# Retention and SwiGLU on one core: a new order for the first batch's transposes and first weights, and six pieces behind each plain down step

## The chip, the core and the metric

The kernel runs on one core of one Trainium2 chip. A core has five engines, each with its own instruction queue: PE (TensorE, matmuls, with a weight load PEld that overlaps them), DVE (VectorE), ACT (ScalarE), POOL (GpSimd) and SP (SyncE, which here only issues DMAs). ACT issues DMAs too. The metric is the device time of one execution in microseconds (us); lower is better.

## The reference

All matrices are float32 but for the three weights, which arrive as float64.

```python
# q, k, v: (8 batches, 8 heads, 576 positions, 64)
scores = (1 / sqrt(64)) * q @ k.transpose(0, 1, 3, 2)
gamma = 1 - 2.0 ** (-5 - arange(8))                  # one decay for each head
Dmat = where(rel >= 0, gamma ** rel, 0)              # rel = query position - key position
ret = (scores * Dmat) @ v
x = ret.transpose(0, 2, 1, 3).reshape(4608, 512)     # tokens x (heads * 64)
g, val = x @ w_gate, x @ w_val                       # 512 -> 1536, each
out = (g * sigmoid(g) * val) @ w_out                 # 1536 -> 512
```

## The kernel before, in words

**Retention.** A unit of work `i` is one pair of heads of one batch (32 units; the first batch is units 0 to 3, and `HP` is 4). Its 576 positions are nine chunks of 64. Inside a chunk the scores are made, masked by `near` and multiplied with v; this is `own_values` (L519). What lies before a chunk comes in as a 64x64 state for each head: `new_states` (L529) makes each chunk's contribution from keys and values on PE, `states` (L573 to L580) chains them on DVE, and `earlier_values` (L540, L544) multiplies the states with the queries. Both kinds of value go to the PSUM tile `outer`; `to_x` (L595, L609) multiplies them out of it into the FFN's input. `masked(i)` returns three closures: `copies` (ACT copies half of the states, `even`), `own` (DVE masks the scores into `ret`) and `states`.

**Transposes.** Scores need q and k with the head dimension on the partitions. For the first batch PE does that: `transposes(i)` turns q into `bankA` and k into `bankB` by four 128x128 transposes each (L464), and the last 64 positions of both into `bankC` (L468). DVE (unit 0) or ACT (units 1 to 3) copies them out to `qT` and `kT` (L465, L471). Then `keys` (L496, L498) scales k in place, which `new_states` needs: on DVE for unit 0, on ACT for unit 1, on POOL for units 2 and 3. Later units are transposed on DVE (`STREAM_TRANSPOSE`, L481). For units 10 and 11 `keys` is on DVE.

**The order of the first batch.** `tick(t, 0, HP)` does, for t = 0 to 5: scores and new states of unit t-1 and their masks; own values, earlier values and `to_x` of unit t-2; then the transposes of unit t. Engines run their queues in the order in which the program issues (a manual schedule).

**Weights.** Each weight block is loaded raw as 64-bit words (`load_w`, L383, L385; 1 MB, three buffers), split by two ACT instructions into its high and low words (`split`, L402, L403) and rounded to float32 by two DVE instructions (`rounding`, L415, L416). `halves` lists the half blocks in the order in which they are rounded; `rounding(j)` issues `split(j+1)` behind itself, and a split of a block's second half issues the load that takes its buffer. Loads 0 to 4 are issued by SP, later ones by ACT. Block 0 is w_gate's and block 1 w_val's for the output blocks 0 and 1, so that the first projection `up0(0)` needs the first halves of both and `up0(1)` the second halves.

**FFN.** The first tile has 512 tokens and plain matmuls: `up0(f)` (L690) for f = 0 to 11, a gate bank and a value bank each, with SiLU on ACT (L694) and the product on DVE (L695); then `down0(f)` (L702) in the order `down_order`. Four more tiles of 1024 tokens follow, in which each quarter of a product is 26 block products by a bilinear scheme (tables UP, DOWN, OUT_SUMS); the sums of blocks that it needs are made on DVE and POOL (L726, through the helper `add`), and some go out to DRAM as DMAs (L777).

**Pieces.** From unit 4 on, `tick` issues the PE work at once and queues the work of the other engines as closures in `pieces`; `go_on(n)` issues the next n. While the plain down steps run, ticks 10, 11 and 12 are queued behind steps m = 1, 3 and 6, one piece is issued at once, and each further step issues five. For ticks 10 and 11 the list is: copies; outputs; own; states; transpose of q; transpose of k; `keys` of units 10 and 11. Behind the pieces, each step issues a group of sums on POOL (`groups`) and one on DVE (`last_groups`).

Of the kernel before, what the change touches and what calls it, by code (L numbers as in the profile page):

```python
# [12 lines left out]
F32 = mybir.dt.float32  # L13
# [141 lines left out]
def kernel(  # L155
# [34 lines left out]
    B, H, S, D = q.shape  # L190
    NT, DM = out.shape
    DF = moe_w_gate.shape[1]
    P = 128
    HP = H // 2
    L = D
    NC = S // L
    NFULL = S // P
    CW = NFULL * P
# [18 lines left out]
    qp = ctx.enter_context(tc.tile_pool(name="qp", bufs=2))  # L217
# [149 lines left out]
        weights.append((src, [w_dn[:, u // 2, 2 * (u % 2) + f].rearrange("p d x -> p (d x)") for f in range(2)]))  # L367
    order = [0, 1, 2, 3, 4, 5, 6, 12, 7, 8, 13, 9, 10, 14, 11, 15, 16, 17]
    assert sorted(order) == list(range(len(weights)))
    halves = [(i, f) for i in order for f in range(2)]  # L370
    RAWS = 3
    raws, parts = {}, {}

    def load_w(m):

        i, queue = order[m], nc.sync if m < 5 else nc.scalar
        raw = rest[:, raw_at + m % RAWS * 2048 : raw_at + (m % RAWS + 1) * 2048]
        raws[i] = raw.bitcast(I32)
        dst, src = raw.bitcast(I64), weights[i][0]
        if i < NUP:  # L380
            dst = dst.rearrange("p (c n) -> p c n", n=2 * P)
            for cols in (ts(0, P), ts(1, P)) if m < 2 else (slice(0, 2 * P),):
                queue.dma_start(out=dst[:, :, cols], in_=src[:, :, cols])  # L383
        else:
            queue.dma_start(out=dst.rearrange("p (f n) -> p f n", f=2), in_=src)  # L385
# [7 lines left out]
    def split(j):  # L393

        i, f = halves[j]
        bits = bits_of(i, f)
        top, ulp = [rest[:, part_at + 512 * (2 * n + j % 2) : part_at + 512 * (2 * n + j % 2 + 1)] for n in range(2)]  # L400
        blocks = lambda a: a.rearrange("p (c m) -> p c m", m=P)
        nc.scalar.activation(out=blocks(top), in_=bits[:, :, :, 1].bitcast(F32), func=AF.Prelu, scale=2.0 ** -112, alpha=2.0 ** 32)  # L402
        nc.scalar.activation(out=blocks(ulp.bitcast(I32)), in_=bits[:, :, :, 0].bitcast(U32), func=AF.Copy, scale=2.0 ** -29)  # L403
        parts[j] = top.bitcast(I32), ulp.bitcast(I32)
        if f and j // 2 + RAWS < len(order):
            load_w(j // 2 + RAWS)

    def rounding(j):

        i, f = halves[j]
        dst = weights[i][1][f].bitcast(I32)
        top, ulp = parts.pop(j)
        nc.vector.tensor_scalar(out=dst, in0=top, scalar1=3, scalar2=None, op0=ALU.logical_shift_left)  # L415
        nc.vector.tensor_tensor(out=dst, in0=dst, in1=ulp, op=ALU.add)  # L416
        if j + 1 < len(halves):
            split(j + 1)

    for m in range(RAWS):  # L420
        load_w(m)

    kT = const.tile([P, S], F32, name="kT")
    state = const.tile([P, NC, D], F32, name="state")
# [2 lines left out]
    spare = rest[:, dn_at + 2560 : sum_at]  # L427
    other = (spare[:, 0:CW].rearrange("p (h c i) -> p h c i", h=2, i=L), spare[:, CW : CW + L],
             spare[:, 640 : 640 + NC * D].rearrange("p (c d) -> p c d", d=D))
    for t in (state, other[2]):  # L430
        nc.gpsimd.memset(t[:, 0], 0.0)

# [19 lines left out]
    def transposes(i):  # L452
        p = i % HP
        qk, kn, vt = loaded.pop(i)
        qT = qp.tile([P, S], F32, tag="qT", name="qT")
        st[i] = dict(qT=qT, kn=kn, v=vt)
        pieces = []

        copy = nc.scalar.copy if i else nc.vector.tensor_copy
        if i < HP:  # L460

            for t, src, bank in ((qT, qk, bankA), (kT, kn, bankB)):
                for c in range(NFULL):
                    nc.tensor.transpose(bank[:, ts(c, P)], src[:, ts(c, P)], ident)  # L464
                copy(t[:, 0:CW], bank)  # L465
            for n, src in enumerate((qk, kn)):
                for hl in range(2):
                    nc.tensor.matmul(bankC[half[hl], ts(n, L)], src[half[hl], CW : CW + D], ident[half[hl], half[hl]],  # L468
                                     start=True, stop=True, skip_group_check=True)
            for n, t in enumerate((qT, kT)):  # L470
                copy(t[:, CW:S], bankC[:, n * L : (n + 1) * L])  # L471
        else:
            if light(i):
                def scale_q():

                    src = qk[:, 0].rearrange("p (j r) d -> p r j d", r=2)
                    for r in range(2):
                        nc.scalar.activation(out=src[:, r], in_=src[:, r], func=AF.Copy, scale=piece[:, 2 * p + r : 2 * p + r + 1])
                pieces.append(scale_q)
            for n, t in enumerate((qT, kT)):  # L480
                pieces.append(lambda n=n, t=t: nc.vector.transpose(out=t, in_=qk[:, n].rearrange("p j d -> p (j d)")))  # L481

        every = slice(0, P)

        def keys():
            blocks = kn.rearrange("p (g d) -> p g d", d=D)
            if i < HP:
                parts = [(0, every, blocks[:, 0 : NC - 1 : 2]), (1, every, blocks[:, 1:NC:2]), (1, half[1], blocks[half[1], NC - 1])]
            elif whole(i):
                parts = [(0, every, blocks[:, 0:NFULL]), (1, every, blocks[:, NFULL:NC])]  # L490
            else:
                parts = [(hl, every, blocks[:, hl : 2 * NFULL : 2]) for hl in range(2)]
            for hl, rows, at in parts:
                scale = key[rows, 2 * p + hl : 2 * p + hl + 1]
                if vector(i) or 1 < i < HP:
                    (nc.vector if vector(i) else nc.gpsimd).tensor_scalar(out=at, in0=at, scalar1=scale, scalar2=None, op0=ALU.mult)  # L496
                else:
                    nc.scalar.activation(out=at, in_=at, func=AF.Copy, scale=scale)  # L498

        if light(i):  # L500
            return [lambda: (keys(), pieces[0]())] + pieces[1:]
        if vector(i) and i:
            return [lambda: None] + pieces + [keys]
        return [keys] + pieces
# [131 lines left out]
    def tick(t, lo=HP, hi=NP, spread=False, then=None):  # L636
        go_on(len(pieces))
        if hi == HP:

            if lo <= t - 1 < hi:  # L640
                scores(t - 1, True)
                new_states(t - 1)
                for f in masked(t - 1):
                    f()
            if t == 3:
                split(0)
                rounding(0)
            if lo <= t - 2 < hi:
                own_values(t - 2)
                earlier_values(t - 2)  # L650
                to_x(t - 2)[0]()
            for f in transposes(t) if lo <= t < hi else ():
                f()
            return
        if lo <= t - 2 < hi:
            own_values(t - 2)
        if lo <= t - 1 < hi:
            new_states(t - 1)
        if lo <= t - 2 < hi:
            earlier_values(t - 2)  # L660
        if lo <= t - 1 < hi:
            scores(t - 1, t - 2 < lo)
        if lo <= t - 1 < hi and whole(t - 2) and not whole(t - 1):
            decay(slice(0, H), slice(0, H), half[1])
        copies, *masks = masked(t - 1) if lo <= t - 1 < hi else (lambda: None,)
        keys, *new = transposes(t) if lo <= t < hi else (lambda: None,)
        outputs = to_x(t - 2)[0] if lo <= t - 2 < hi else lambda: None
        if t - 2 >= 0 and light(t - 2):
            pieces.append(lambda: (copies(), keys(), outputs()))
        else:  # L670
            pieces.extend([lambda: (copies(), keys()), outputs])
        pieces.extend(masks)
        pieces.extend(new)
        if then:
            pieces.append(then)
        if not spread:
            go_on(len(pieces))

    def go_on(n):
        for _ in range(min(n, len(pieces))):  # L680
            pieces.pop(0)()
# [303 lines left out]
    for t in range(HP + 2):  # L985
        tick(t, 0, HP)

        for j in {3: (1, 2), 4: (3, 4, 5)}.get(t, ()):
            rounding(j)
        if t == 3:  # L990
            load(HP)
        if t > 3:
            for f in range(2):
                up0(f, range(2) if t == 4 else range(2, HP))
    load(HP + 1)


# [36 lines left out]
    tick_at = {1: 10, 3: 11, 6: 12, 8: 13}  # L1034
    for m, f in enumerate(down_order):
        down0(f)
        go_on(5)
        if m in tick_at:
            tick(tick_at[m], HP, FIRST, tick_at[m] + 1 < needed(1))
            go_on(1)  # L1040
        if m == 8:
            first_sums(0, 0, 4)
        if m > 8:
            x_sums(1, 3 * (m - 9), min(3 * (m - 8), X_FIRST), True)
        if groups:
            groups.pop(0)[1]()
        if last_groups:
            last_groups.pop(0)()
# [58 lines left out]
```

## Time and profile before

| what | value |
|---|---|
| median of 4 runs | 1066.01 us (1064.81 to 1067.23) |
| the profiled execution | 1065.88 us |
| its span, first to last instruction | 1064.1 us |
| PE busy | 1039.0 us (98%) |
| DVE, POOL, ACT busy | 663.2, 390.0, 273.7 us |
| first transposes on PE start | 4.17 us |
| plain up projections `up0` | 30.64 us to about 129 us |
| plain down steps `down0` | 129.24 us to about 187 us |
| mean granted TensorE clock | 0.998 |

Read it so: a row of the timeline gives the start and the duration of a group of like instructions on one engine; in brackets stands how long the engine was idle before it and what released it. The view of waits sums these for each pair of waiting and releasing instruction (us in total, times, the longest). "SPq" and "ACTq" are instructions that issue DMAs. A PE row's end is modelled: it holds the last matmul's way through the array, so that rows of work in sequence overlap a little.

### The profile page before, as it was taken

Reading aid. Unit: us, or ns where it says so; the run is one execution under the profiler, and the core shown is the slowest. Engines: PE = TensorE matmul, PEld = TensorE weight load, DVE = VectorE, ACT = ScalarE, POOL = GpSimd, SP = SyncE. Lnnn points to the kernel's source line nnn. Section 1 sums busy time; section 2 is a strip of 40 time slices with the busy share of each in tenths; the row PEclk is TensorE's granted clock in tenths of the full one; section 3 lists DMA queues with packets and bytes.
Section 4 is the critical chain, followed back from the end, with each engine's and each line's share of the span. In section 5 each row is a group of like instructions: output and inputs, shape, how many; then the busy total and the mean of one; then the engine's idle time right before and its main releaser. Section 6 shows DMA issues by size and latency. Waiting matters only on the chain.

```text
span 1064.1 us, 21426 instructions
## 1 busy us (share of the span) xinstructions
PE 1039.0 (98%) x8448; PEld 851.3 (80%) x8448; DVE 663.2 (62%) x1094; ACT 273.7 (26%) x579; POOL 390.0 (37%) x338
## 2 busy tenths in 40 slices
PE   6999989999999999999999999999999999999998
PEld 5554545888887888888888888888888888888887
DVE  5568778886878678463557778526375554244644
ACT  4456400333433210332322112232220022222110
POOL 2002356656455206621224037512250384122505
PEclk9999999999999999999999999999999999999999
DMA  9898788746768968756766867554554555555553
GB/s 272 212 281 231 195 240 227 218 143 191 187 178 217 263 166 230 212 154 182 192 161 192 220 190 212 155 151 137 151 176 155 155 179 157 150 154 160 182 159 98
DMA packets 305083, 199.09 MB, mean 187 GB/s; under 512 B 219992, under 2 KB 248664, under 8 KB 304984
## 3 DMA queue, kind: packets, MB, share of 16 engines
q1 hardware_dynamic: 269528, 157.19, 54.0%
q10 hardware_dynamic: 35456, 40.54, 11.3%
q8 instruction: 67, 1.10, 0.4%
q14 instruction: 32, 0.26, 0.1%
HBM read 157.56 MB, written 40.11 MB: 186 GB/s over the span
## 4 chain that ended last, share of the span: by engine, by line
PE 84%; DVE 8%; DMA 2%; issue 2%; POOL 1%; ACT 0%; ACTq 0%; DVEq 0%; POOLq 0%
PE bankC L919 11%; PE bankE L919 11%; PE bankB L919 11%; PE bankA L919 11%; PE bankA L958 6%; PE bankB L958 6%; PE bankE L958 6%; PE bankC L958 6%; DVE rest L859 3%; PE bankA L690 2%; PE outer L544 2%; PE bankC L690 2%; PE bankE L690 2%; PE bankB L690 2%; DVE rest L726 2%
## 5 line engine op out<-in xcount | busy, mean ns | idle before, releaser
L859 POOL TENSOR_TENSOR rest<-rest 128x512 f32<-128x512 f32 x56 | 79.2, 1420 | 298.5 <-DVE rest L859 277.5
L934 ACT ACTIVATE io<-rest 128x256 f32<-128x256 f32 x180 | 75.0, 417 | 342.3 <-DVE rest L859 294.2
L919 PE MATMUL bankC<-rest,arena 128*128 128x256 f32 x544 | 129.2, 380 | 0.5 <-DVE rest L859 0.5
L919 PE MATMUL bankA<-rest,arena 128*128 128x256 f32 x544 | 129.0, 380 | 0.6 <-DVE rest L859 0.6
L726 POOL TENSOR_TENSOR arena<-arena 128x512 f32<-128x512 f32 (+1 forms) x72 | 114.1, 1597 | 32.2 <-DMA up<-arena 21.0
L919 PE MATMUL bankE<-rest,arena 128*128 128x256 f32 x512 | 121.4, 380 | 0.6 <-DVE rest L859 0.6
L919 PE MATMUL bankB<-rest,arena 128*128 128x256 f32 x512 | 121.5, 380 | 0.4 <-DVE rest L859 0.4
L919 PEld LDWEIGHTS bankA<-rest,arena 128*128 128x128 f32 x544 | 102.9, 190 | 16.1 <-issue 1.4
L919 PEld LDWEIGHTS bankC<-rest,arena 128*128 128x128 f32 x544 | 102.8, 190 | 15.6 <-issue 1.2
L941 POOL TENSOR_TENSOR arena<-rest,io 128x256 f32<-128x256 f32 x72 | 52.0, 729 | 166.6 <-ACT io L934 166.6
L919 PEld LDWEIGHTS bankE<-rest,arena 128*128 128x128 f32 x512 | 96.9, 190 | 14.5 <-DVE rest L859 1.0
L919 PEld LDWEIGHTS bankB<-rest,arena 128*128 128x128 f32 x512 | 96.9, 190 | 14.5 <-DVE rest L859 0.8
L726 POOL TENSOR_TENSOR rest<-rest 128x256 f32<-128x256 f32 (+1 forms) x66 | 66.1, 1022 | 102.5 <-DVE rest L416 59.9
L859 DVE TENSOR_TENSOR rest<-bankC,rest 128x512 f32<-128x512 f32 x72 | 48.9, 687 | 65.4 <-PE bankC L919 45.1
L859 DVE TENSOR_TENSOR rest<-bankB,rest 128x512 f32<-128x512 f32 x72 | 48.9, 687 | 64.3 <-PE bankB L919 49.3
L859 DVE TENSOR_TENSOR rest<-bankE,rest 128x512 f32<-128x512 f32 x72 | 48.8, 686 | 63.6 <-PE bankE L919 45.4
L859 DVE TENSOR_TENSOR rest<-bankA,rest 128x512 f32<-128x512 f32 x72 | 48.8, 686 | 63.5 <-PE bankA L919 46.2
L937 DVE SCALAR_TENSOR_TENSOR arena<-rest,io 128x256 f32<-128x256 f32 x84 | 57.4, 688 | 11.7 <-ACT io L934 11.7
L958 PE MATMUL bankA<-arena 128*128 128x256 f32 x252 | 58.0, 380 | 1.4 <-DVE arena L726 1.4
L958 PE MATMUL bankB<-arena 128*128 128x256 f32 x252 | 58.3, 381 | 0.0
L958 PE MATMUL bankC<-arena 128*128 128x256 f32 x252 | 58.1, 380 | 0.0
L958 PE MATMUL bankE<-arena 128*128 128x256 f32 x252 | 57.9, 379 | 0.0
(180 smaller groups left out, 1632.5 us busy)
## 6 DMA issues: line engine op xcount, KB each, us to landing
arena<-up SPq DMA_DIRECT2D x234, 256.0 KB, 2.6
arena<-dn SPq DMA_DIRECT2D x104, 384.0 KB, 3.1
up<-arena ACTq DMA_DIRECT2D x78, 256.0 KB, 3.0
out_dram<-rest SPq DMA_DIRECT2D x32, 256.0 KB, 3.7
qk<-in_q_dram SPq DMA_DIRECT2D x108, 72.0 KB, 2.6
qk<-in_k_dram SPq DMA_DIRECT2D x108, 72.0 KB, 2.3
dn<-rest SPq DMA_DIRECT2D x52, 128.0 KB, 2.4
rest<-in_moe_w_out_dram ACTq DMA_DIRECT2D x6, 1024.0 KB
```

The lines of the kernel that those rows point to most:

```text
L544: nc.tensor.matmul(xr[half[hl]] if c + 1 == NC else xo[half[hl ^ c % 2 * exchange(i)], c // 2, c % 2], state[half[hl], c, :], s["qT"][half ...
L690: nc.tensor.matmul(bank, w_up[:, f // 4, gv, f % 4, c // 2, (c % 2) * P : (c % 2 + 1) * P], xs[0][:, c, :], start=(c == 0), stop=(c == HP ...
L726: eng.tensor_tensor(out=dst, in0=srcs[0], in1=srcs[1], op=ALU.add if op[0] == "add" else ALU.subtract)
L859: eng.tensor_tensor(out=at(op[1]), in0=at(op[2]), in1=at(op[3]), op=ALU.add if op[0] == "add" else ALU.subtract)
L919: nc.tensor.matmul(b[:, gv * TB : (gv + 1) * TB], w[:, gv, ts(c, P)], rhs[:, c, :], start=(opens and gv == 0 and c == 0), stop=(c == 1), s ...
L934: nc.scalar.activation(out=s, in_=src[:, 0:TB], func=AF.Silu, scale=-1.0 if negative else 1.0)
L937: return lambda: nc.vector.scalar_tensor_tensor(out=dst, in0=src[:, TB : 2 * TB], scalar=-1.0, in1=s, op0=ALU.mult, op1=ALU.mult)
L941: nc.gpsimd.tensor_tensor(out=dst, in0=src[:, TB : 2 * TB], in1=s, op=ALU.mult)
L958: nc.tensor.matmul(b[:, m * TB : (m + 1) * TB], lhs[:, qd, ts(m, P)], w[:, qd], start=(opens and qd == 0 and m == 0), stop=(qd == NQ - 1), ...
```

## The change

Three things are changed, and nothing is added to what is computed.

1. *The first batch's ticks.* The transposes of unit t now stand between own values and earlier values of unit t-2. For units 1 to 3, k is transposed and copied ahead of q, and each tensor's last 64 positions follow its own 128x128 transposes. The first four `qT` have places of their own (`early`) in a part of `rest` that is not yet in use.
2. *The first two weight blocks.* They are loaded and rounded by columns: first half of gate, first half of value, then the two second halves. The roundings are spread otherwise over the ticks (0 at t = 3; 1 between `own` and `states` of t = 4; 2 behind t = 4; 3, 4, 5 behind t = 5; before: 0, 1, 2 at t = 3 and 3, 4, 5 at t = 4). `up0(0)` has its first two input chunks behind t = 4 and the other two behind t = 5; `up0(1)` then runs whole. Loads 3 and 4 are tied to the splits of the second halves; on SP's queue they now come behind the ten DMAs of `load(4)`, unit 4's q, k and v, which they were ahead of.
3. *The plain down steps* issue six pieces each instead of five.

```diff
-    halves = [(i, f) for i in order for f in range(2)]
+    halves = [(i, f) for f in range(2) for i in order[0:2]] + [(i, f) for i in order[2:] for f in range(2)]
...
-    def load_w(m):
+    def load_w(m, parts=range(2)):
...
-            for cols in (ts(0, P), ts(1, P)) if m < 2 else (slice(0, 2 * P),):
+            for cols in [ts(f, P) for f in parts] if m < 2 else (slice(0, 2 * P),):
...
-        if f and j // 2 + RAWS < len(order):
-            load_w(j // 2 + RAWS)
+        m = j + 1 if 1 < j < 4 else j // 2 + RAWS
+        if f and m < len(order):
+            load_w(m)
...
-    for m in range(RAWS):
-        load_w(m)
+    for f in range(2):
+        for m in range(2):
+            load_w(m, (f,))
+    load_w(2)
...
+    early = [spare[:, 640 + S * (1 + i) : 640 + S * (2 + i)] for i in range(HP)]
...
-        qT = qp.tile([P, S], F32, tag="qT", name="qT")
+        qT = early[i] if i < HP else qp.tile([P, S], F32, tag="qT", name="qT")
...
-            for t, src, bank in ((qT, qk, bankA), (kT, kn, bankB)):
+            for n, (t, src, bank) in enumerate(((kT, kn, bankB), (qT, qk, bankA)) if i else ((qT, qk, bankA), (kT, kn, bankB))):
                 for c in range(NFULL):
                     nc.tensor.transpose(bank[:, ts(c, P)], src[:, ts(c, P)], ident)
-                copy(t[:, 0:CW], bank)
-            for n, src in enumerate((qk, kn)):
                 for hl in range(2):
                     nc.tensor.matmul(bankC[half[hl], ts(n, L)], src[half[hl], CW : CW + D], ident[half[hl], half[hl]],
                                      start=True, stop=True, skip_group_check=True)
-            for n, t in enumerate((qT, kT)):
-                copy(t[:, CW:S], bankC[:, n * L : (n + 1) * L])
+                copy(t[:, 0:CW], bank)
+                copy(t[:, CW:S], bankC[:, ts(n, L)])
...
-                for f in masked(t - 1):
-                    f()
-            if t == 3:
-                split(0)
-                rounding(0)
+                copies, own, states = masked(t - 1)
+                copies()
+                own()
+                if t == HP:
+                    rounding(1)
+                states()
             if lo <= t - 2 < hi:
                 own_values(t - 2)
+            for f in transposes(t) if lo <= t < hi else ():
+                f()
+            if lo <= t - 2 < hi:
                 earlier_values(t - 2)
                 to_x(t - 2)[0]()
-            for f in transposes(t) if lo <= t < hi else ():
-                f()
...
-        for j in {3: (1, 2), 4: (3, 4, 5)}.get(t, ()):
+        if t == 3:
+            split(0)
+        for j in {3: (0,), 4: (2,), 5: (3, 4, 5)}.get(t, ()):
             rounding(j)
         if t == 3:
             load(HP)
-        if t > 3:
-            for f in range(2):
-                up0(f, range(2) if t == 4 else range(2, HP))
+        if t == 4:
+            up0(0, range(2))
+    up0(0, range(2, HP))
+    up0(1, range(HP))
...
         down0(f)
-        go_on(5)
+        go_on(6)
```

## The prediction

> **What bounds the kernel now.** I read the busy shares first, then the view of waits for PE, then windows for the clock, then the timelines of the two places that the change touches.
>
> ```profile
> span 1064.1 us, 21426 instructions
> ...
> PE 1039.0 (98%) x8448; PEld 851.3 (80%) x8448; DVE 663.2 (62%) x1094; ACT 273.7 (26%) x579; POOL 390.0 (37%) x338
> ```
>
> PE is busy for all but 25 us. So only what shortens PE's own gaps, or makes its matmuls faster, can count. PE's waits in full come to under 20 us, and these are the ones that the change can reach:
>
> ```profile
> PE inner L529 <- DVE kn L496: 3.3, 3, 2.6
> PE inner L529 <- POOL rest L496: 2.3, 2, 1.6
> ...
> PE bankE L552 <- ACT kT L471: 1.6, 3, 0.6
> ```
>
> The first lies in the plain down steps, the other two in the first batch: new states wait for scaled keys, scores for the copies of the transposes. A wait can also cost clock:
>
> ```profile
> 25.54:28.95 3.41, 1.74 (x78) 1.47 (x74) 2.45 (x6) 2.49 (x5) 1.74 (x2) 0.99 0.99 351
> 28.95:32.37 3.42, 3.42 (x36) 2.40 (x33) 3.28 (x12) 0.72 (x2) 0.00 (x0) 0.51 1.02 340
> 32.37:35.78 3.41, 3.41 (x9) 1.52 (x8) 2.69 (x5) 2.80 (x5) 0.00 (x0) 1.00 0.90 123
> ```
>
> Columns: stretch, its length, busy time of PE, PEld, DVE, ACT, POOL, granted clock, DMA share, GB/s. After a stretch in which PE worked 1.74 of 3.41 us, the clock was 0.51 for 3.42 us. The rest of the run shows no other such dip.
>
> **The first batch, part by part.** The timeline of the third tick and the fourth:
>
> ```profile
> 18.24 0.27 PE L552 MATMUL bankE<-qT,kT 64*64 64x64 f32 x2 [0.58 <-ACT kT L471]
> ...
> 19.82 0.63 PE L529 MATMUL inner<-v,rest 64*64 64x64 f32 x27 [0.67 <-POOL rest L496]
> ...
> 24.83 0.27 PE L552 MATMUL bankE<-qT,kT 64*64 64x64 f32 x2 [0.58 <-ACT kT L471]
> ...
> 27.43 0.63 PE L529 MATMUL inner<-v,rest 64*64 64x64 f32 x27 [1.59 <-POOL rest L496]
> ```
>
> *Removed.* Transposes now come before earlier values, so that 0.33 + 0.93 us of PE work (L540, L544) stands between the last transpose and the scores. The ACT copies end about 0.75 us after the last transpose; that work hides them, and two waits of 0.58 go: 1.16. Were it gone, they would be back.
>
> POOL starts `keys` when k's transposes end. Unit 2's scaling took 17.39 to 19.77 (2.38 us for three instructions). Now k is transposed right behind own values of unit 0, which end near 14.8: its four transposes end 0.66 later, POOL runs 15.5 to 17.9, and PE reaches the new states near 14.8 + 1.7 (transposes) + 1.25 (earlier values) + 0.55 (scores) = 18.3. No wait: 0.67 goes. For unit 3 the same sum from own values ending at 19.4 gives POOL 20.1 to 22.5 and PE at 22.9: 1.59 goes. The old row for unit 3 is 3.35 us, beside rounding on DVE from 23.5 on, which now begins after `to_x` of unit 1, near 23.2. With 3.35 PE would wait 0.6; I take 2.38, the row without rounding, and keep 0.6 for the range.
>
> [...] The old rows show the stretch only beside rounding, so my sum leaves it out.
>
> Earlier values wait until own values have left the array (0.21 us between PEld rows, twice in ticks 2 and 3); transposes now fill that: 0.4.
>
> *The clock.* PE's hole at 25.84 to 27.43 closes, so the half-clock stretch should go. Its price: L544 took 1.71 us on the chain against 0.93 later, and the first four rows of `up0` 2.72 against 1.72 for the next four: 1.7 to 1.8; I take 1.7. Bounds: 0 if any 3.4 us stretch stays as empty as that one, 1.8 if not. The stretch 18.7 to 22.1 was some 0.66 busy and caused no dip, and every new stretch from 14 us on comes out above that, so I take the full value.
>
> [...]
>
> *Added.* The last 64 positions of the second tensor go into the bank that the first one's copy has to leave, and in the changed program PE waits for it: ACT's 0.49 + 0.22 behind the first transposes, against 0.5 of transposes that cover it: 0.2 in each of ticks 1 to 3, and earlier values are queued behind it: 0.6. No row shows this wait; bounds 0 to 1.5 (three times 0.5, both tensors' copies in full). In tick 0 k's copy comes behind q's small one: 0.2.
>
> *First weights.* `up0(0)` and `up0(1)` keep their matmuls. Between own values of units 2 and 3 stand now 3.44 us of `up0` instead of 6.88. In that time DVE has to do the mask (0.6), rounding 1 (1.1), the states (2.0) and `to_x` (0.85) = 4.55, against PE's own values 0.6 + earlier values 1.1 + 3.44 = 5.15, with ACT's copy of 0.4 ahead: cover 0.2. ACT's two splits stand ahead of that copy, up to 1.2 us. I charge 0.4, bounds 0 to 1.4. The DMA of gate's and value's first halves comes in the order of use; ACT splits at 21 us in both.
>
> SP passes `load(4)` ahead of load 3. SP was free at 18.67 and `load(4)` took 27.93 to 39.34 = 11.4 us to issue; from 18.7 that is 30.1, and a weight load of 1 MB took 5.6 to 6.1 us to land: near 36. Its split, behind which the first SiLU is queued on ACT, then takes 2 x 0.6, the table load 1.28, SiLU 0.60, DVE's product 0.69: 39.8, and `up0(2)` needs that bank near 43.3. Cost 0, with 3.5 us of cover.
>
> Sum: 1.16 + 0.67 + 1.59 + 0.4 + 1.7 - 0.6 - 0.2 - 0.4 = **4.3 us** saved. `up0(2)` starts at 43.5 instead of 47.82. From there to 129 us PE shows no wait, and each engine's queue hangs on PE as before. Ends: 1.1 (no clock, added terms at their bounds) to 5.7.
>
> **Six pieces.** The timeline of DVE, then of PE, around unit 10's keys:
>
> ```profile
> 144.95 0.73 DVE L481 STREAM_TRANSPOSE kT<-qk 128x576 f32<-128x576 f32 x1
> 145.61 2.98 DVE L726 TENSOR_TENSOR rest<-rest 128x256 f32<-128x256 f32 x4
> 148.51 1.64 DVE L496 TENSOR_SCALAR kn<-kn,tab 128x256 f32<-128x256 f32 x2
> ```
>
> ```profile
> 146.08 0.69 PE L519 MATMUL outer<-ret,v 64*64 64x64 f32 x32
> 149.38 0.33 PE L529 MATMUL inner<-v,kn 64*64 64x64 f32 x2 [2.60 <-DVE kn L496]
> 150.21 0.63 PE L529 MATMUL inner<-v,kn 64*64 64x64 f32 x27 [0.51 <-DVE kn L496]
> ```
>
> Four sums stand between the transpose and the keys. The sixth piece is `keys`, so it changes places with them: it starts at 145.6 instead of 148.5, 2.9 us sooner, and PE gets its keys at 147.3 instead of 150.2. What is late next is still `keys`, by 0.7 against a pass without wait. For unit 11 three sums (2.13 us) step aside; own values to L540 took 1.75 there against 0.98 in the tick at 126.5, so 0.8 goes. The sums now delay DVE's `even` copy: they end at 150.2, PE has its states ready at 149.6, and PE does not need that copy's results before 160. The sums' DMAs to DRAM leave ACT's queue 1.6 us later; the later tiles fetch them only behind their up steps. POOL's groups keep their places. Tick 12 has four pieces and is untouched. Sum 2.9 + 0.8 = **3.7 us**; with DVE slowed by POOL 2.6, at most 4.3 (all delay of the two passes).
>
> **Where it could leak.** In 190 to 290 us PE has waits of 0.3 to 0.8 us for DVE and POOL, so DVE must come early too. It does: it idles 2.42, 1.75 and 0.92 us for PE at 152.6, 166.6 and 176.0, the last just before it starts the first big tile's sums. POOL idles 3.3 us at 177.8. I charge 0, with 2 us as the bad end.
>
> Total 4.3 + 3.7 = 8.0. The profiled execution is 1065.88, span 1064.1; so 1065.88 - 8.0 = **1057.9 us** (span 1056.1). The median of the runs is 0.13 above the profiled one, which I neglect.
>
> **Rivals.**
> *Half of the first batch's gain is lost:* the clock dips again and own values of unit 3 wait for `to_x`. The cover of 0.2 us speaks for it; the closed hole against. Gain 1.1 to 2.6 + 3.7: 1059.6 to 1061.1, middle 1060.4. Chance 0.17.
> *The shift does not pass the first big tile:* DVE or POOL there set the end. Their bracketed waits for PE speak against. If half of the gain stays behind: 1062; if nearly all, no change. Chance 0.10.
> *Slower: load 3 late.* SP's waits show one DMA of a later unit standing 9.9 us behind a weight load. If `load(4)` stands so ahead of load 3, that lands near 46.5; PE stalls from 39.5 on, by 7 us, and a hole of that length brings half clock for one or two stretches, 1.7 to 3.4 more. From a landing at 47.5 on, the stall alone eats the whole gain. 1057.9 + 7.0 + 3.4 = 1068.3. Against it: no ACT-issued load stands among the DMAs that load 3 follows. Chance 0.05.
> The forecast itself: 0.68.
>
> **How the numbers follow.** A measurement of this kernel tells 0.2% (2.1 us) from no change. Faster: 0.68 + 0.17 + 0.06 of the second rival's 0.10 (most of the ways to split it lie beyond 2.1 us) = 0.91; same 0.04 (the rest of it); slower 0.05. The forecast's own spread is +-2 (1.1 for added waits, 0.6 for keys, 1 for the six pieces), 1055.9 to 1059.9; with the first rival's whole span and part of the second the range is 1055.4 to 1061.4.
>
> **What would show it.** Right: no PE wait on POOL's keys, the clock at 1.00 from 12 us on, `up0(2)` near 43.5, PE's wait for DVE's keys under 0.6 in all, `down0` ending near 179. Wrong: a clock stretch near 0.5 after 14 us; `outer` L519 waiting for `to_x`; ACT's SiLU waiting for a weight DMA at 36 to 45; or PE's waits in 180 to 290 grown by over 2 us.

## The result: 0.35% faster, half of the forecast

| | before | after |
|---|---|---|
| median | 1065.39 us (63 runs) | 1061.37 us (44 runs) |
| ratio | | 0.9965 (95%: 0.9957 to 0.9973) |
| profiled execution, span | 1065.88, 1064.1 us | 1059.96, 1058.2 us |
| `up0(2)` starts (timeline) | 47.65 us | 46.35 us |

Forecast were 8.0 us; 4.0 came by the medians (1065.39 - 1061.37), 3.7 by the ratio. The page of the changed kernel:

```profile
span 1058.2 us, 21432 instructions
...
PE 1037.9 (98%) x8448; PEld 850.8 (80%) x8448; DVE 662.1 (63%) x1094; ACT 273.5 (26%) x579; POOL 389.7 (37%) x338
```

Its waits on PE:

```profile
PE outer L521 <- DVE arena L416: 2.4, 1, 2.4
...
PE outer L521 <- issue: 0.5, 1, 0.5
...
PE inner L531 <- DVE kn L498: 0.3, 1, 0.3
```

The 3.3 us for DVE's keys are 0.3, the 2.3 us for POOL's are gone. The first row is new: own values of unit 2, 2.4 us. In PE's timeline of the third and fourth tick:

```profile
20.38 0.68 PE L521 MATMUL outer<-rest,v 64*64 64x64 f32 x26
21.56 0.34 PE L521 MATMUL outer<-rest,v 64*64 64x64 f32 x6 [0.51 <-issue]
...
25.11 0.68 PE L531 MATMUL inner<-v,rest 64*64 64x64 f32 x32
28.16 0.69 PE L521 MATMUL outer<-ret,v 64*64 64x64 f32 x32 [2.36 <-DVE arena L416]
```

No wait in front of L531 and none in front of scores, as forecast; but PE stands directly behind that work. The named releaser, a rounding on DVE, writes no operand of own values. Note also the 0.51 us of "issue" in the middle of a run of equal matmuls, 26 rows in and 6 to go. The kernel before has the same mark at the same place, which the prediction did not take up:

```profile
21.16 0.34 PE L519 MATMUL outer<-rest,v 64*64 64x64 f32 x6 [0.30 <-issue]
```

The six pieces, DVE first:

```profile
144.71 1.08 DVE L498 TENSOR_SCALAR kn<-kn,tab 128x256 f32<-128x256 f32 x2
145.70 3.14 DVE L730 TENSOR_TENSOR rest<-rest 128x256 f32<-128x256 f32 x4
```

```profile
144.78 0.69 PE L521 MATMUL outer<-ret,v 64*64 64x64 f32 x32
...
146.25 0.22 PE L542 MATMUL outer<-ret_last,v 64*64 64x64 f32 x1
```

Keys stand ahead of the four sums. Own values to earlier values took 1.47 us (4.55 before), and 0.98 in the next tick (1.75): 3.1 + 0.8 = 3.9.

### The profile page after: what moved, and what is told of

It reads as the page before. It is cut to its first block, busy times and chain, and to the rows that moved or that the text cites. A ratio compares the mean times of both kernels' runs of the same rounds, so it can differ in the third digit from the quotient of the medians.

```text
span 1058.2 us, 21432 instructions
## 1 busy us (share of the span) xinstructions
PE 1037.9 (98%) x8448; PEld 850.8 (80%) x8448; DVE 662.1 (63%) x1094; ACT 273.5 (26%) x579; POOL 389.7 (37%) x338
## 4 chain that ended last, share of the span: by engine, by line
PE 84%; DVE 8%; DMA 3%; issue 2%; POOL 1%; ACT 1%; SPq 0%; ACTq 0%; DVEq 0%; POOLq 0%
PE bankC L923 11%; PE bankE L923 11%; PE bankB L923 11%; PE bankA L923 11%; PE bankA L962 6%; PE bankB L962 6%; PE bankE L962 6%; PE bankC L962 6%; DVE rest L863 3%; PE bankA L694 2%; PE bankC L694 2%; PE outer L546 2%; PE bankE L694 2%; PE bankB L694 2%; PE outer L521 2%
```

## The experiments

Ratios are against the kernel before, run on the same chip, with the 95% interval.

### The two parts apart

e1: `go_on(5)` becomes `go_on(6)` in the kernel before. e2: the reverse in the changed kernel.

> The kernel before with six pieces behind a plain down step in place of five, and nothing else. The forecast's term for it is 3.7 us; the rows of the changed kernel (own values to earlier values 1.47 and 0.98 us, against 4.55 and 1.75 before) say 3.9. So 0.9963 to 0.9965 of the time before if the shift passes the first big tile whole; near 0.998 if half of it stays behind there; about 1.000 if the whole difference of the two kernels came from the first batch.

> The changed kernel with five pieces again, so the first batch's change alone. By the forecast 4.3 us less (0.996). The difference measured for the whole change, 4.0 us, less 3.7 to 3.9 for the six pieces, leaves 0.1 to 0.3 us (0.9997 to 1.000); the profiled pair, in which up0(2) starts 1.3 us sooner, leaves 1.3 us (0.9988).

e1: 0.9980 (0.9959 to 1.0001), some 2.1 us. e2: 0.9994 (0.9976 to 1.0012), some 0.6 us. `up0(2)` started at 48.25 us in e2, later than before. The six pieces come out below 3.7 us, but 3.7 lies within the interval (0 to 4.4 us); the first batch misses its 4.3 us by more than the interval, which ends at 2.6.

### What the new stall is

Theory W takes the row at its word: PE waits for DVE. Theory F starts from the list of DMA queues:

```profile
q8 instruction: 67, 1.10, 0.4%
```

Packets, MB, share. PE runs 8448 weight loads, 8448 matmuls and 402 others: 17,298 instructions, and 1.10 MB / 17,298 is 64 bytes for each. So these 67 packets of 16 KB should be PE's own program, 256 instructions apiece, and each packet the fetch of one such block (e3 below has 64 instructions more, and 68 packets). In the trace's DMA records one ran from 25.75 to 26.84 us, just ahead of the end of the stall.

```
+    nc.vector.memset(ret[:, 0, 0], 0.0)
+    for _ in range(16):
+        nc.tensor.matmul(bankE[half[0], 0:8], ret[half[0], 0, 0], ret[half[0], 0, 0, 0:8], start=True, stop=True)
     for t in range(HP + 2):
```

> The changed kernel with 16 matmuls of 64 x 8 zeros ahead of the first transposes, in the time in which PE has no input yet; one memset of 64 x 64 on DVE ahead of them. Theory F: the idle 2.36 us ahead of own values of unit 2 (28.16 us) come from PE's instruction stream, which the trace shows being fetched in blocks of 16 KB, one of them from 25.75 to 26.84 us; the padding puts 64 more instructions into the stream, so every block ends 32 PE rows sooner in the work, and the stall moves ahead of new states of unit 3 or is covered by queued work. Theory W: own values of unit 2 wait for something on DVE (the rounding that the row names, or an order behind own values of unit 3); the stall then stays ahead of them, 2.0 to 2.6 us long, with the same line named. Time: W the same as the changed kernel within 0.3 us; F anything from 2 us less to 1 us more.

```profile
22.72 0.64 PE L560 MATMUL inner<-rest,kT 64*64 64x64 f32 x30
26.51 1.14 PE L531 MATMUL inner<-v,rest 64*64 64x64 f32 x32 [3.15 <-issue]
```

The stall went 32 rows ahead, to the first of the new states, and nothing waits at own values. 16 x 4 instructions of padding are 32 rows: F. Counted from the start of PE's records, the first instruction after the gap is number 961 in both kernels, and in the changed one the gap of 0.51 us stands at number 705, 256 before, as the 0.30 us does in the kernel before. Time 0.9945 (0.9924 to 0.9965); it can't be laid to one thing, since the padding also keeps PE busy from 1.04 us on and moves every later fetch.

### Why the fetch is late

e5 moves `load(HP)` from tick 3 to tick 4, behind weight loads 3 and 4. e6 does the reverse in the kernel before. e9 is e5 with weight load 2 also held back:

```
-    load_w(2)
...
+        if t == 4:
+            load_w(2)
```

e12 is e9 with the second halves of the first two weights issued by ACT at the end of tick 2.

> The changed kernel with the loads of unit 4 behind weight loads 3 and 4 on SP, where the kernel before has them; PE's, DVE's and ACT's orders are the changed kernel's. The padding showed that the stall sits at one fixed place of PE's instruction stream, behind the fetch of the next 16 KB. Theory F1: that fetch is late (25.75 us, with PE at its last instruction, where other fetches start 130 to 220 instructions ahead) because unit 4's loads, whose first piece SP issues at 19.16 us, stand in the DMA engines ahead of it. Then the fetch starts 1.5 to 2.5 us sooner here, the 2.36 us of idle time shrink to 0.6 or less, and up0(2) starts 1.5 to 2.5 us sooner. Theory F2: the fetch is late whatever the loads do, since PE reaches the end of the block too fast after its last wait: 2.0 to 2.6 us of idle time as before, time within 0.3 us of the changed kernel.

> The kernel before with the loads of unit 4 ahead of weight loads 3 and 4 on SP, as the changed kernel has them, and nothing else. F1: the fetch that started at 24.92 us moves to 26 or later, and PE, which stands at POOL's keys until 27.43 anyway, gets a second stall of 0.5 to 2 us some 30 rows later; 0.5 to 2 us more time. F2: the fetch stays within 0.5 us of its place and nothing changes.

> The kernel of the run with unit 4's loads late, and in it weight load 2 (1 MB) also behind weight load 3 on SP; no order on PE, DVE or ACT changes. There the DMA engines were full (share 1.07) to 25.7 us and idle behind that, and PE's fetch started at 25.37, with the last of the three weight loads. Theory F1: the fetch stands behind the weight loads' transfers; without the third of them the engines are free some 3 us sooner, the fetch starts within 1.2 us of PE's entering the block before it (about 22.5 to 23 us), PE's stall behind new states of unit 3 (1.77 us there) falls to 0.5 or less, and up0(2) starts 1.3 to 2 us sooner. Theory F2: the fetch comes 3.5 us or more behind that entry whatever the transfers do; the stall stays at 1.5 to 2.5 us. Rival G: load 2 now lands too late and ACT's splits or up0(2) wait for it: a stall of 1 us or more between 35 and 50 us.

> The kernel with weight load 2 and unit 4's loads late, and in it the second halves of the first two weights (512 KB each) too: ACT issues them behind its copies of the third tick, where SP issued them at 16.7 us. PE's order is unchanged. Left over there was a stall of 1.15 us at the second fetch (block from instruction 705 on). F1: that stall, too, is the fetch standing behind weights; with only two halves on the way the fetch starts 0.9 to 1.2 us after PE enters the block before, and the stall falls to 0.6 or less, but not to nothing, since PE runs these 256 instructions in about 3.3 us and the shortest fetch seen takes 1.0 us to start and 2.4 more until PE goes on; the third fetch may lose 0.5 us to the later halves. up0(2) at 44 to 44.7 us. F2: 1.1 to 2.3 us stay at the second fetch.

DMA share and GB/s are the last two columns of the stretches; e5 first, then e9:

```profile
22.00:24.00 2.00, 2.00 (x32) 1.46 (x29) 1.62 (x5) 1.08 (x3) 1.11 (x2) 1.00 1.08 372
24.00:26.00 2.00, 2.00 (x102) 1.95 (x96) 1.00 (x4) 1.98 (x5) 1.25 (x2) 1.00 0.86 312
```

```profile
22.00:24.00 2.00, 1.46 (x17) 1.16 (x18) 1.89 (x7) 0.44 (x1) 0.38 (x1) 1.00 0.67 209
24.00:26.00 2.00, 2.00 (x76) 1.77 (x76) 0.28 (x3) 1.88 (x6) 1.91 (x3) 1.00 0.02 8
```

And PE, e5 then e9:

```profile
25.37 0.71 PE L531 MATMUL inner<-v,rest 64*64 64x64 f32 x32
27.85 0.69 PE L521 MATMUL outer<-ret,v 64*64 64x64 f32 x32 [1.77 <-DVE arena L417]
```

```profile
22.54 0.34 PE L520 MATMUL outer<-rest,v 64*64 64x64 f32 x6 [1.15 <-issue]
...
26.11 0.82 PE L530 MATMUL inner<-v,rest 64*64 64x64 f32 x29
26.79 0.67 PE L520 MATMUL outer<-ret,v 64*64 64x64 f32 x31
```

With 1 MB fewer on the way the engines ran empty near 23.2 us instead of 25.5, and the stall at instruction 961 is gone (e15 below, with the same loads, has none there either); the one at 705 is 1.15 us, against 0.78 in e5. `up0(2)` starts at 44.94 us, against 46.04. The DMA records give more. A share is the packets' time over that of 16 engines; packets overlap, so it can pass 1 (1.09 in the first row). "Entry" is the moment at which PE begins instruction 705; the fetch is that of the block from 961 on:

| kernel | fetch starts after entry | DMA share in the 2 us ahead | 705 to 961 takes | idle at 961 |
|---|---|---|---|---|
| before | 3.76 us | 1.09 | 6.7 us | none |
| after | 4.19 | 1.07 | 6.59 | 2.36 us |
| e2 | 4.02 | 1.08 | 6.59 | 2.40 |
| e3 | 4.83 | 1.09 | 7.43 | 3.15 |
| e5 | 3.56 | 1.07 | 6.05 | 1.77 |
| e9 | 1.33 | 0.70 | 4.2 | none |

This fetch took 0.9 to 1.4 us, and where PE stood for it, it went on 1.2 to 1.6 us behind its end. Among the first five fetches of all profiles, those with a DMA share of 0.70 or less ahead of them started 0.5 to 1.5 us after entry. With a full share the third fetch started 3.1 to 4.8 us after it in all but one (1.69, in e15, whose DMA engines ran empty just then, at 23.3 us). Fetches of the block from 705 on sometimes started within 1 us under a share of 0.85 to 1.0, so here a full share made a late fetch likely, not certain. That what is queued ahead of it decides is an argument; the records don't show it.

So e5's F1 was mostly wrong (0.6 us instead of 1.5 to 2.5): unit 4's loads are not the main thing ahead of the fetch; by e9 against e5 it is weight load 2. e6 agrees: fetch at 3.70 us after entry, time 0.9997 (0.9980 to 1.0014). e5 came to 0.9928 (0.9907 to 0.9949), e9 to 0.9949 (0.9936 to 0.9961) on another chip, with the changed kernel beside it:

> The changed kernel itself, beside the two others on the same chip, for the comparison between them: 0.9965 of the kernel before, within the interval; the fetch behind new states of unit 3 starts when PE is at the end of its block, and PE stands for 2.0 to 2.6 us, whatever the place of the clock's steps.

That was 0.9969 (0.9956 to 0.9982), median 1061.84 us against 1059.15 for e9: holding back the loads is worth 2.7 us in medians of 6 and 5 runs, and 3.0 in the pair e14 and e15 below, which differs by the same loads (1062.83 against 1059.85). Part of that is clock: the runs' mean granted clock was 0.9977 against 0.9990, and 0.9974 against 0.9994, or 1.4 and 2.1 us. How much the weight brings and how much unit 4's loads, the times don't tell: e5 gained as much on its chip, with its stall of 1.77 us. The profile of e11 differs from its expectation:

```profile
19.24 0.68 PE L521 MATMUL outer<-rest,v 64*64 64x64 f32 x26
22.18 0.48 PE L521 MATMUL outer<-rest,v 64*64 64x64 f32 x6 [2.27 <-issue]
```

The same program stood at instruction 705 this time, and not at 961. The clock of the same profile in stretches that end with its steps:

```profile
18.67:22.08 3.41, 1.24 (x68) 1.05 (x60) 2.66 (x9) 0.37 (x1) 0.00 (x0) 1.00 0.95 314
22.08:25.49 3.41, 3.31 (x26) 2.41 (x28) 0.32 (x1) 0.99 (x3) 1.62 (x2) 0.50 1.05 379
25.49:28.91 3.42, 3.42 (x100) 3.42 (x101) 1.22 (x4) 2.76 (x6) 0.65 (x2) 0.50 0.90 184
28.91:32.30 3.39, 3.29 (x89) 2.46 (x82) 3.15 (x7) 2.88 (x5) 0.00 (x0) 1.00 0.59 95
```

The hole left 1.24 of 3.41 us of work, and two stretches at half clock followed. In them the next fetch, though it started 3.95 us after entry, ended 1.75 us before PE began its block, and PE did not stand.

e12 missed: 3.17 us of idle time at 705, fetch 3.58 us after entry at a share of 1.09. ACT issued the halves at 16.9 and 17.3 us, just when that fetch was due (entry 16.7). That agrees with F1, but the forecast was wrong; time 0.9949 (0.9930 to 0.9968).

### The new order alone

e8 is the kernel before with the changed `transposes` and tick order only.

> The kernel before with the new order of the first batch's transposes alone (k ahead of q, transposes between own and earlier values, the second tensor's rest in the first's bank); first weights, their loads and up0 as before. The forecast's terms for this part: 1.16 for copies, 2.26 for POOL's keys, 0.4 for the row halves, less 0.8: 3.0 us less, and 1.7 more where the clock does not dip. F1, with unit 4's loads late: no stall of PE at the third fetch; 2 to 4 us less. F2: the stall of 2.0 to 2.6 us stands there; 0 to 1.5 us less.

0.9989 (0.9972 to 1.0006), 1.2 us: less than F1 forecast, within F2's 0 to 1.5, but without the stall at the third fetch on which F2 rests. Its profile has a wait that the whole change doesn't have:

```profile
24.65 0.33 PE L467 MATMUL bankC<-ident,rest 64*64 64x64 f32 x4 [2.41 <-ACT kT L470]
```

This is the wait for the bank that the first tensor's copy has to leave, which the prediction charged with 0.2 us a tick: where ACT splits weights ahead of its copies, it costs 2.41 us. In the changed kernel `split(0)` stands behind the copies and the wait is nowhere to be seen. So the moved splits look needed for the order's worth; but here too the fetch for 961 lay under the wait (it ended at 25.72 us), and no run parts the two.

### The cold start

PE's rows were slow at first: in the changed kernel's profile 32 rows of new states took 1.17 us at 14.55 us, in its repetition 27 took 0.63 at 14.28. e4, e7, e10 and e13 keep PE busy before the first input:

```
+    nc.vector.memset(ret, 0.0)
+    zero = ret.rearrange("p r c i -> p (r c i)")
+    for _ in range(2):
+        nc.tensor.matmul(bankE, zero[:, 0:P], zero, start=True, stop=True)
```

> The changed kernel with two matmuls of 128 x 512 zeros (four PE rows) ahead of the first transposes, so that PE is busy from about 1 us instead of 4.4 us. Theory C: PE's slow rows at the start (states 1.17 us for 32, against 0.68 later) last until PE has been busy long enough, which was at 16.5 us in the changed kernel's profile; the dummies bring that forward to 8 to 12 us, and 8 us of rows at 1.17 / 0.68 shrink by 2 to 3.5 us, of which PE's waits for copies at the start take some back: 1.5 to 3 us less time. Rival: the start hangs on the inputs, ACT's and DVE's copies, not on PE's rate: 0, or 0.3 us more where the dummies still run when the first input is there.

> The changed kernel with both: two matmuls of zeros ahead of the first transposes, and unit 4's loads behind weight loads 3 and 4. The dummies alone brought up0(2) from 46.5 to 43.9 us in their profile, with a stall of 2.5 us left. F1: that stall goes too, up0(2) starts near 42, and the time is 6.5 to 8 us below the kernel before. F2: the stall stays, up0(2) at 43.5 to 44.5, 4.5 to 5.5 us below the kernel before.

> The same with two matmuls of 128 x 512 zeros ahead of the first transposes. F1: PE at full clock from 8 us on or earlier, no stall over 0.5 us at the third fetch, up0(2) at 41.5 to 43 us (44.67 in the run with the dummies and unit 4's loads late), and the median 6 to 8 us below the kernel before. F2: up0(2) at 43.5 to 45 us, 5 to 6 us below.

> The same with two matmuls of 128 x 512 zeros ahead of the first transposes. If the fetches and the clock are all that ate the first batch's gain, this has neither stall nor clock step: up0(2) at 41.5 to 43 us, or where ACT's splits behind load 2 (done near 41 us) hold it, 42.5 to 43.5; median 6 to 8 us below the kernel before (0.9925 to 0.9944). If a clock step of 3.4 us remains, up0(2) at 44 to 45 and 4.5 to 6 us below.

PE was fast from 4 to 8 us on in all four profiles, and `up0(2)` started at 43.94, 44.67, 44.32 and 46.55 us. Yet the times are not clearly better than without the dummies, and e7, e10 and e13 fall short of the 6 to 8 us that were expected of them without a stall: e4 0.9954 (0.9935 to 0.9974), e7 1059.89 against 1059.89 for e5, e10 1060.73 against 1059.15 for e9, e13 1063.99 against 1061.41 for e12. Theory C is right for the start and wrong for the time. PE reaches the end of a block sooner, but the fetch is as late after entry as before (4.30 us in e4), and it stands there:

```profile
22.46 0.68 PE L531 MATMUL inner<-v,rest 64*64 64x64 f32 x27
25.67 0.27 PE L531 MATMUL inner<-v,rest 64*64 64x64 f32 x2 [2.52 <-issue]
```

(e4; e13 stood 3.02 us, and its clock was halved from 24.9 to 31.7 us.)

### Where six pieces lose

In e1 own values to earlier values took 1.61 and 0.99 us, 2.9 + 0.8 less than before: the forecast's terms. Still its time moved by 2.1 us only. ACT's copy of bank A at the end of the plain down steps, before, after, and after again:

```profile
183.96 0.59 ACT L708 COPY rest<-bankA 128x512 f32<-128x512 f32 x1 [4.85 <-PE bankA L702]
```

```profile
178.85 0.59 ACT L712 COPY rest<-bankA 128x512 f32<-128x512 f32 x1 [1.73 <-PE bankA L706]
```

```profile
182.57 0.59 ACT L712 COPY rest<-bankA 128x512 f32<-128x512 f32 x1 [0.64 <-DMA dn<-rest]
```

Before, ACT stood ready 4.85 us ahead of PE. PE now comes some 5 us sooner (178.85 against 183.96 us in the first two rows). ACT is ready 2 us sooner in the one profile and later in the other: 1.73 us are left, or nothing, and then PE waits for the bank:

```profile
183.21 1.99 PE L923 MATMUL bankA<-rest,arena 128*128 128x256 f32 x8 [1.25 <-ACT rest L712]
```

Of 13 profiles with six pieces 6 show this wait, 1.25 to 2.09 us long (e1 1.49), and all 6 show POOL waiting 1.5 to 2.9 us, between 148 and 156 us, for a store to land; the 5 in which POOL waited 0.9 us or less show none (2 more, with 1.55 and 2.09 us, got by). e14 and e15 give POOL three buffers of DVE's:

```
-    vector_places = x0_places + more_places[6:] + ...
+    vector_places = x0_places + more_places[9:] + ...
...
-                    plan.append(lambda places=more_places[:6]: pool_places.extend(places))
+                    plan.append(lambda places=more_places[:9]: pool_places.extend(places))
```

> The changed kernel with three buffers more for POOL's sums (15 in place of 12), taken from those of DVE's sums (19 in place of 22); no order changes on any engine. In the profiles of the kernels with six pieces, those in which POOL waits about 2 us near 154 us for a store to land before it can write its next sum (1.96, 2.24, 2.07 and 2.90 us in four of them) show PE waiting 1.25 to 1.49 us at the first big tile for ACT's copy of bank A, and those in which POOL waits 0.5 us or not at all show none. Theory L: POOL's wait is for a buffer, and it makes the late sums, ACT's activation and ACT's copies late; with three buffers more POOL waits under 0.6 us, PE does not wait for ACT at 180 us, and the median falls by 0.5 to 1.5 us against the changed kernel. Rival: what POOL waits for is not a buffer, or DVE, with three fewer, now waits in its place; 1.2 to 2.1 us of waiting for ACT stay in this profile or the median does not move.

> The kernel with weight load 2 and unit 4's loads late, with POOL's three buffers more. L: both losses are gone, 0.9935 to 0.9950 of the kernel before and no PE wait for ACT near 180 us; rival: the same as with the late loads alone, 0.9949.

```profile
155.09 0.81 POOL L727 TENSOR_TENSOR rest<-rest 128x256 f32<-128x256 f32 x1 [2.73 <-DMA dn<-rest]
```

e14: POOL still waits, PE waits 1.50 us for ACT, 0.9980 (0.9963 to 0.9998). Theory L falls: three more buffers do not end POOL's wait. e15, whose profile has neither wait, came to 0.9950 (0.9929 to 0.9972), the same as e9. That the cover of 4.85 us is used up, and that PE then waits for ACT, is shown; why that store lands late in some executions stays open.

## Why the prediction was half right

**Six pieces, 3.7.** Right in place: 3.9 in the pair of profiles, 3.7 in e1. The failed step is "Where it could leak", charged 0 with 2 us as the bad end. It looked for idle time of DVE and POOL and did not name ACT, whose copies stand in its queue behind the sums' DMAs. The second rival ("does not pass the first big tile", 0.10) is partly what happened, with ACT in place of DVE or POOL: 1.25 to 2.09 us in 6 of 13 profiles. Its chance was too small. The times alone do not show this loss (e1's interval holds 3.7); the profiles show the wait.

**POOL's keys, 0.67 and 1.59.** The waits went as forecast, and the scaling took 2.44 and 2.41 us beside DVE's states, so the value without stretch was the right one. The failed step is the worth of the second. In the kernel before, instructions 705 to 961 took 6.7 us, with ACT's wait of 0.58 and POOL's of 1.59 among them. In the changed kernel's profile they took 6.59, without either. The fetch for 961 ended at 25.97 us in the old trace and PE, waiting for POOL, went on at 27.43: the fetch lay under the wait all along. Where PE stood for a fetch it went on 1.2 to 1.6 us behind its end, so it could not have begun 961 before 27.2 to 27.6 us, and it did so at 27.9. The sum asked "what is late next" of the engines alone; this resource has no name in the view of waits. e9, without a stall at 961, shows the terms were otherwise sound: 4.2 us.

**The copies, 1.16, and row halves, 0.4.** Waits gone as forecast; of the part in the fourth tick the same holds.

**The clock, 1.7.** What was read from the old row came again. Count stretches of 3.41 us from the clock's own steps, over the first 45 us of all profiles: of those at full clock, nine with 0.95 to 1.86 us of PE's work were followed by half clock and none with 1.94 or more; three with 1.80 to 1.85 were not. The failed step is "every new stretch from 14 us on comes out above that": it assumed that the hole closes, and it moved. In the profile of after it lay across two stretches (2.43 and 1.94 us of work) and cost nothing; in its repetition one stretch was left with 1.24 us of work, and two at half clock followed. Nor was the dip a fixed cost of the kernel before: in e1, whose first batch is the same program, POOL's second wait was 0.77 us instead of 1.59, and the clock stayed full from 17.8 to 352 us. From instruction 961 to `up0(2)` PE took 18.2 us at full clock in both kernels (e1 and after), and 19.8 where the dip fell into it (before and e2), so 1.6 is its price. How much came on average stays open: the mean clock was 0.9987 in the 44 runs after and 0.9968 in the 97 runs of the kernel before beside the experiments, or 2.0 us, but 0.9977 against 0.9975 on one chip (e11), and e1, e3, e6, e8 and e10 show dips of the same length between 149 and 353 us, too.

The prediction also took the start for constant: full speed from 11.8 us in the old profile, from 16.5 in the new, from 11.8 in its repetition.

**Added terms, 1.2, and load 3.** The bank's order wait cost nothing here (2.41 in e8). The first weights' 0.4 do not show either: own values of unit 3 start at 33.77 us without a wait. ACT splits from 24.1 us on, not from 21, which the prediction took for both kernels. Load 3 came later than the forecast's 36 us (ACT, waiting for it, began its split at 40.15), and the cover took that up: no stall at `up0(2)`.

**The first rival.** Its 1059.6 to 1061.1 us come nearest to the measured 1061.4. The clock did dip in some executions, but own values of unit 3 do not wait for `to_x`; that the number is near is partly luck.

Together, in the pair of profiles: the terms that act before instruction 961 promise 3.0 us (1.16 + 0.67 + 1.59 + 0.4 - 0.6 - 0.2), but PE began 961 at 28.16 us instead of 27.9, 0.3 later. The others promise 1.3 (1.7 - 0.4) and brought 1.6. So the 1.3 us by which `up0(2)` starts sooner are the clock's, and what is missing went ahead of 961: to 2.87 us of standing for fetches, against 0.30, and to the later full clock. That is one pair. Of the 4.0 us that the medians miss, the first big tile takes about 0.7 by the profiles (1.5 us in about half of them); the rest is not parted by any run.

## What to carry to other kernels

When a wait of PE in a stretch of small matmuls is to go, look in the list of DMA queues for the instruction queue and in the trace for the time of its packets: 256 instructions of such work last 2.6 to 4.2 us here, about as long as a fetch with the DMA engines free (1.1 us to its start, 1.0, and 1.4 until PE goes on), and less than most with them full (3.1 to 4.8 us to the start). Loads that nobody needs yet belong behind such a stretch: here that was worth 2.7 and 3.0 us more than without (e9 against e11, e15 against e14).
And before time is taken out ahead of a handover, list the slack of every engine that must have finished there, ACT's queue with its DMAs included.

## What was not expected of the hardware

PE's program streams in as 67 packets of 16 KB. In the first 50 us a packet started 0.5 to 1.5 us after PE entered the block before, where the DMA engines' share ahead of it was 0.70 or less; with full engines the third started up to 4.8 us after. PE stood for up to 3.17 us.

In the changed kernel's profile 64 of the 66 fetches that the count of PE's records reaches ended 2.3 us or more before PE began their block. For the two others, both in the first batch, PE stood 0.51 and 2.36 us; wherever a run shows a stall at one of these two places, it is 0.3 to 3.2 us long.

The row "<- DVE arena L416" was no such wait, and "issue" was no property of the instruction: both were the missing program. A releaser that writes no operand of the waiting instruction is a reason to count instructions.
